# Moving an SSM kernel's parameter columns to a transposing DMA, its stores to ScalarE and one skip product to VectorE

**Chip, cores, metric.** One core of one Trainium2 chip. The metric is the device time of the kernel in microseconds, median of several runs. All results were correct. Starts, waits and clocks are read from one profiled run of each kernel.

## The reference

For 2048 tokens of width 448 (bf16): normalize `x` to `xn`, run a diagonal complex state space model over the tokens, multiply its output by a gate from a gated MLP (1792 hidden columns), add `x`.

```python
xn = layernorm(x)
# A: state space model, 448 complex states
h_t = Lam_bar * h_(t-1) + B_bar @ xn_t            # Lam_bar = exp(exp(log_dt) * Lambda)
s   = 2 * Re(C @ h) + xn * Dskip                  # xn * Dskip is "the skip"
# B: gated MLP
g = silu((silu(xn @ w_gate) * (xn @ w_up)) @ w_down)
out = x + s * g
```

The parameters `log_dt`, `Lambda_re`, `Lambda_im` and `Dskip` are rows of 448 in memory. The kernel needs them as columns, one state to a partition.

## The kernel before

The tokens go through in four blocks of 512 (`q`), each of four tiles of 128 (`j`). The order on TensorE is gate and up products (`gu`, tiles `gp`, `up`), input products of the model (`pb`), output sums (`y`) and down products (`hd`). Where the argument below needs a block, it says pb(2) or hd(1). The recorded texts also call the input products `bu`: the third bu is pb(2). Tile names in the profile: `gs` and `us` are gate and up copied out of PSUM, where TensorE's matmuls write; `Vt` is their product, which the down products read; `sg` is the SiLU of `hd`; `ob` is the output tile; a "notice" is the message between the shares. TensorE runs "cold" when its granted clock shows 0.50, half rate.

The matmul groups. Each contraction is cut into two shares that use two halves of the array (64*128 in the profile; a gate and an up product start together). The program lets the second share of a pair start only when the first share is done. That order goes through GpSimd: an empty instruction there waits for TensorE, and TensorE waits for it.

```python
def tell(mm):
    told = nc.gpsimd.nop(nofuse=True)                       # stands in GpSimd's queue
    tc.add_manual_dep(told.ins, mm.ins.name, SYNC, reason="share")
    return told.ins.name

def sums(q, pairs, between=None):                           # cut
    for share, first in ((0, True), (1, False)):
        for n, two in enumerate(pairs):
            ...                                             # matmuls of this share
                if not first and m == 0:
                    told_of(mm, left[n])                    # second share waits for the notice
            if first:
                left.append(tell(mm))
        if first:
            run_power()                                     # queues one pow on GpSimd
```

The layer norm of later blocks: ScalarE makes the sums (`act_sum`, with tile `junk`), GpSimd the root, on the same queue as those notices.

```python
def act_root(q):                                            # cut
    nc.gpsimd.tensor_scalar(out=vep[...], in0=sums_of[:, 1, :], ...)
    nc.gpsimd.tensor_tensor(out=rstd[...], in0=vep[...], in1=halves[:], op=ALU.pow)
    nc.gpsimd.tensor_tensor(out=off_of[:, 1, :], in0=off_of[:, 0, :], in1=rstd[...], op=ALU.mult)
```

The start, where the parameter columns come out of tile 3's transposes:

```python
def second_tokens():
    ln_evacuate(2, ln_transpose(2), nc.scalar)              # tile 2: PSUM -> xT by ScalarE
    t = ln_transpose(3)
    tv = params_row(t)                                      # six tiny TensorE transposes
    ln_evacuate(3, t, nc.vector)
    nc.scalar.activation(pcol[:], tv, ACT.Copy)             # the columns
    power(dtv[:], euler[:], pcol[:, 0:KT, 0])               # first user, on GpSimd
```

The middle of the program:

```python
    turned_norms(8, 9, 10, 11)                              # ScalarE norms, SyncE transposing DMAs
    outs(0, sg)                                             # outputs of block 0, stores on SyncE
    sg = downs(1, 2.4, {                                    # hd(1)
        0: act_sums((12, 13, 14), 0) + [on(skips, 2)],
        1: act_sums((15,), 0) + [act_means] + act_sums((12, 13), 1),
        2: act_sums((14, 15), 1) + [on(act_root, 3)],
    })
    drive(2, 4.8)                                           # pb(2), scans
    gu(2, bg, 2.4)
```

Of the kernel before, what the change touches and what calls it, by code (L numbers as in the profile page):

```python
# [10 lines left out]
ALU = mybir.AluOpType  # L11
ACT = mybir.ActivationFunctionType
BF16 = mybir.dt.bfloat16
# [31 lines left out]
def kernel(  # L45
# [43 lines left out]
    def blk(k):  # L89
        return slice(k * P, k * P + P) if k < KF else slice(D - P, D)  # L90

    def block(n):
        return slice(n * P, (n + 1) * P)
# [13 lines left out]
    def ctile(shape, dtype, name):  # L107
        return const.tile(shape, dtype, name=name)
# [13 lines left out]
    Id = ctile([P, P], BF16, "Id")  # L122
    CT = ctile([P, KT, W], BF16, "CT")
    ST = ctile([P, KT, W], BF16, "ST")
    vrow = ctile([4, D], BF16, "vrow")
    xn = [ctile([P, KT * P], BF16, f"xn{i}") for i in range(TQ)]
    pcol = ctile([P, KT + 1, 4], F32, "pcol")
    it_f = work.tile([P, W], F32, name="it_f", tag="row", bufs=1)
# [40 lines left out]
    natC = [work.tile([P, KT, D], BF16, name="natC", tag="nz") for _ in range(2)]  # L169
    nc.vector.memset(Wd[:, 0, :], 0.0)  # L170
    nc.vector.memset(Id[:], 0.0)
    nc.vector.memset(half_pi[:], math.pi / 2)
    for h, v in ((slice(0, R), TWO_PI), (slice(R, P), -TWO_PI)):
        nc.vector.memset(two_pi[h], v)

    def warm(n):
        t = bank("warm")
        for _ in range(n):
            nc.tensor.matmul(t[:, 0:D], lhsT=Wd[:, 0, 0:P], rhs=Wd[:, 0, :], start=True, stop=True)
# [51 lines left out]
    vep = ctile([P, NT], F32, "vep")  # L231
    rstd = ctile([P, NT], F32, "rstd")

    def ln_stats(n):
        st = work.tile([P, nc.vector.BN_STATS_DIM], F32, name="st")
        nc.vector.bn_stats(out=st[:], in_=x_all[:, n, :])
        nc.vector.bn_aggr(out=mv[:, n, :], in_=st[:])
        nc.vector.tensor_scalar(
            out=vep[:, n : n + 1], in0=mv[:, n, 1:2], scalar1=1e-5, scalar2=None, op0=ALU.add
        )  # L240
# [15 lines left out]

    sums_of = ctile([P, 2, TQ], F32, "sums_of")
    off_of = ctile([P, 2, TQ], F32, "off_of")

    def act_sum(n, squares):  # L260
        i = n % TQ
# [33 lines left out]
    def ln_transpose(n):  # L295
        tp = bank("tp", BF16)
        for k in range(KT):
            nc.tensor.transpose(tp[:, block(k)], xn[n][:, blk(k)], Id[:])
        return tp

    def ln_evacuate(n, tp, eng):
        tp = tp[:, 0 : KT * P].rearrange("p (k c) -> p k c", k=KT)
        if eng is nc.scalar:
            nc.scalar.activation(xT_of(n), tp, ACT.Copy)  # L304
        else:
            nc.vector.tensor_copy(out=xT_of(n), in_=tp)
# [9 lines left out]
    dtv = vnew("dtv")  # L316
    b_re, b_im, nb_im = vnew("b_re"), vnew("b_im"), vnew("nb_im")

    def transpose_state(out, src, k, ident):

        if k < KF:
            nc.tensor.transpose(out, src[:, blk(k)], ident)
        else:
            for h in (slice(0, R), slice(R, P)):
                nc.tensor.transpose(out[h], src[:, KF * P : D], ident)

    def params_row(t):

        tv = t[:, KT * P : KT * P + 4 * (KT + 1)].rearrange("p (k r) -> p k r", r=4)
        for k in range(KT + 1):  # L330
            if k < KT:
                transpose_state(tv[:, k, :], vrow, k, Id[0:4, 0:4])
            else:
                nc.tensor.transpose(tv[:, k, :], vrow[:, blk(KF)], Id[0:4, 0:4])
        return tv

    def params_in():
        tt, ts = nc.vector.tensor_tensor, nc.vector.tensor_scalar
# [36 lines left out]
    def params_out():  # L375
        tt, ts = nc.vector.tensor_tensor, nc.vector.tensor_scalar
        ab = pcol[:, 0:KT, 1:3].rearrange("p k c -> p c k")
        tt(out=lam[:], in0=lam[:], in1=rcol[:].unsqueeze(1).to_broadcast([P, 3, KT]),
           op=ALU.mult)
        ts(out=lam[:, 1, :], in0=lam[:, 1, :], scalar1=1.0, scalar2=None, op0=ALU.subtract)  # L380
        tt(out=prod[:, 0:2, :], in0=lam[:, 1:3, :], in1=ab, op=ALU.mult)
        tt(out=nb[:, 0, :], in0=prod[:, 0, :], in1=prod[:, 1, :], op=ALU.add)
        tt(out=prod[:, 0:2, :], in0=lam[:, 0:2, :], in1=ab, op=ALU.mult)
        tt(out=nb[:, 1, :], in0=prod[:, 0, :], in1=prod[:, 1, :], op=ALU.subtract)
        tt(out=b_re[:], in0=nb[:, 0, :], in1=rden[:], op=ALU.mult)
        tt(out=b_im[:], in0=nb[:, 1, :], in1=rden[:], op=ALU.mult)
        ts(out=nb_im[:], in0=b_im[:], scalar1=-1.0, scalar2=None, op0=ALU.mult)
# [215 lines left out]
        return sg  # L603

    skip = {}
    SKIPS = [(q, j) for q in (1, 2, 3) for j in range(TQ)][:-1]

    def skips(q):

        skip[q] = work.tile([P, TQ, D], BF16, name="skip", tag="nz")  # L610
        for j in range(TQ):
            for c0, c1, x0 in ((0, KF * P, 0), (KF * P, D, KF * P + R)):
                nc.vector.tensor_tensor(
                    out=skip[q][:, j, c0:c1], in0=xn[j][:, x0 : x0 + c1 - c0],
                    in1=skip["row"][:, c0:c1], op=ALU.mult,
                )

    def out_sum(q, j, k0=0, k1=KT):

# [34 lines left out]
    def on(fn, *args):  # L654
        return lambda: fn(*args)
# [4 lines left out]
        run_power()  # L660
    for n in range(2):
        ln_norm(n)
        ln_evacuate(n, ln_transpose(n), nc.scalar)
        warm(1 + n)
    for n in range(2, TQ):
        ln_stats(n)
        ln_root(n, n + 1)
    run_power()
    powers.append(count_tokens)

    def second_tokens():
        ln_evacuate(2, ln_transpose(2), nc.scalar)
        t = ln_transpose(3)
        tv = params_row(t)
        ln_evacuate(3, t, nc.vector)
        nc.scalar.activation(pcol[:], tv, ACT.Copy)
        power(dtv[:], euler[:], pcol[:, 0:KT, 0])

    CW = W // 2
# [37 lines left out]
    def drive(q, budget):  # L717
        bu_alloc(q)
        bu(q, (0, 1, 2), True, [on(table_sin, 3), params_trig] if q == 0 else ())
        if q == 0:  # L720
            params_out()
        ssm_steps(bg, q)
        bg.run(budget)

    def downs(q, budget, hooks={}, n=TQ):
        sg = []
        for j in range(n):
            sg.append(down(q, j))
            for fn in hooks.get(j, ()):
                fn()  # L730
            bg.run(budget)
        return sg

    def outs(q, sg, hooks={}):
        for j in range(len(sg)):
            finish(q, j, out_sum(q, j), sg[j])
            for fn in hooks.get(j, ()):
                fn()

    def do(fns):  # L740
        for fn in fns:
            fn()

    gu(0, bg, 0.0, {
        0: [*stats(4, 5), on(params_in), on(table_phase, 0)],
# [15 lines left out]
    def act_sums(ns, squares):  # L761
        return [on(act_sum, n, squares) for n in ns]

    gu(1, bg, 2.2, {2: cw(0)[0], 3: cw(0)[1], 4: cw(1)[0], 5: cw(1)[1]})
    drive(1, 4.0)
    sg = downs(0, 1.8, {
        0: cw(2)[0] + cw(3)[0] + act_sums((8, 9), 0),
        1: act_sums((10, 11), 0) + [act_means] + act_sums((8, 9), 1) + cw(2)[1] + cw(3)[1],
        2: act_sums((10, 11), 1) + [on(act_root, 2), on(skips, 1)],
    })  # L770
    bg.finish(0)
    turned_norms(8, 9, 10, 11)
    outs(0, sg)
    sg = downs(1, 2.4, {
        0: act_sums((12, 13, 14), 0) + [on(skips, 2)],
        1: act_sums((15,), 0) + [act_means] + act_sums((12, 13), 1),
        2: act_sums((14, 15), 1) + [on(act_root, 3)],
    })
# [1 line left out]
    gu(2, bg, 2.4)  # L780
    bg.finish(1)
    turned_norms(12, 13, 14, 15)
    outs(1, sg)
    sg = downs(2, 2.4, {1: [on(skips, 3)]})
    drive(3, 4.8)
    gu(3, bg, 2.4)
    bg.finish(2)
# [36 lines left out]
```

## Time and profile before

| | |
|---|---|
| time, median of 3 (range) | 187.45 us (186.88 to 187.54) |
| span of the profiled run | 185.0 us |
| TensorE busy | 177.9 us |
| output sums y(0) start | 72.27 |
| input products pb(2) start | 89.04 |
| last matmul ends | 181.16 |

The last three rows are read from TensorE's timeline, and such starts of groups are the ruler of this document: where the distance between two of them changes, time was lost or won there. The lines that carry the argument on the bound stand in the prediction below. One more view mattered, and the prediction did not read it. It is GpSimd's timeline of the kernel before around pb(2); columns are start, length, engine, line, operation, and in brackets the idle time before it with what ended it.

```profile
88.44 0.39 POOL L274 TENSOR_SCALAR vep<-sums_of 128x4 f32<-128x4 f32 x1 [11.50 <-ACT junk L263]
88.92 1.01 POOL L278 TENSOR_TENSOR rstd<-vep,halves 128x4 f32<-128x4 f32 x1
90.00 0.22 POOL L281 TENSOR_TENSOR off_of<-off_of,rstd 128x4 f32<-128x4 f32 x1
```

GpSimd is almost idle here, yet it stands 11.50 us waiting for ScalarE's sums.

### The profile page before, as it was taken

The page shows a single profiled execution, that of the slowest core. Times are in us where ns is not written, and L with a number is a line of the kernel's source. Part 1 is how long each engine was busy: PE and PEld are TensorE (multiplying, and loading weights), DVE is VectorE, ACT ScalarE, POOL GpSimd, SP SyncE. Part 2 cuts the span into 40 slices and gives each one's busy share as a digit, 9 for nine tenths or more (in the row PEclk, how much of TensorE's full clock was granted, in tenths as well). Part 3 has the DMA queues.
Part 4 walks back from the last instruction along what each step waited for, and adds up shares of the span by engine and source line. Part 5 has one row for each costly group of instructions (what it writes and reads, how often), then busy time and mean ns, then how long its engine had stood idle before and what let it go on. Part 6 is the DMA issues. An engine that isn't in the chain of part 4 may idle for free.

```text
span 185.0 us, 3723 instructions
## 1 busy us (share of the span) xinstructions
PE 177.9 (96%) x1449; PEld 87.8 (47%) x1449; DVE 160.1 (87%) x254; ACT 120.2 (65%) x247; POOL 13.4 (7%) x25
## 2 busy tenths in 40 slices
PE   7899999999999999999999999979999999999991
PEld 3574444544444555555454444535454444455551
DVE  4649799999999999902999999999999999999583
ACT  3247879997789999498499556962259696512110
POOL 7332200000000000600300000000000000000000
PEclk9999999999999999999999999999999999999999
DMA  5899655979200000043100000042100000001111
GB/s 160 209 277 338 124 94 112 132 167 377 101 0 0 5 0 0 0 86 81 50 2 4 2 0 4 0 82 70 62 4 0 0 4 0 0 4 50 50 50 50
DMA packets 26129, 12.71 MB, mean 69 GB/s; under 512 B 16000, under 2 KB 26112, under 8 KB 26112
## 3 DMA queue, kind: packets, MB, share of 16 engines
q1 hardware_dynamic: 24896, 12.06, 25.3%
q10 hardware_dynamic: 1088, 0.41, 0.8%
q8 instruction: 11, 0.18, 0.4%
q14 instruction: 6, 0.05, 0.1%
q0 software_dynamic: 128, 0.00, 0.0%
HBM read 7.23 MB, written 1.84 MB: 49 GB/s over the span
## 4 chain that ended last, share of the span: by engine, by line
PE 67%; DVE 25%; DMA 3%; issue 2%; ACT 1%; POOL 0%; SPq 0%; DVEq 0%
PE gp L455 20%; PE hd L597 16%; PE up L455 15%; PE pb L455 9%; PE y L626 7%; DVE bu_re L527 5%; DVE bu_im L527 4%; DVE tmp L521 2%; DVE Vt L589 2%; DVE ob L648 2%; DMA out_dram<-ob 2%; DVE t L645 2%; DVE H_im L521 2%; DVE ere L521 1%; DMA x_all<-in_A_x_dram 1%
## 5 line engine op out<-in xcount | busy, mean ns | idle before, releaser
L455 PE MATMUL gp<-xT,Wg 64*128 64x512 bf16 (+1 forms) x413 | 85.8, 365 | 0.4 <-ACT xT L304 0.3
L455 PE MATMUL up<-xT,Wu 64*128 64x512 bf16 (+1 forms) x413 | 85.8, 365 | 0.0
L455 PEld LDWEIGHTS <-Wg 64*128 64x128 bf16 x413 | 38.5, 94 | 25.1 <-issue 0.4
L455 PEld LDWEIGHTS <-Wu 64*128 64x128 bf16 x413 | 38.4, 94 | 19.7 <-POOLq L437 0.5
L581 ACT ACTIVATE gs<-gp 128x512 bf16<-128x512 f32 x56 | 33.7, 604 | 19.6 <-PE gp L455 11.7
L597 PE MATMUL hd<-Wd,Vt 128*128 128x448 bf16 x224 | 43.4, 353 | 1.3 <-DVE Vt L589 1.3
L585 ACT ACTIVATE us<-up 128x512 bf16<-128x512 f32 x54 | 32.9, 609 | 0.0
L597 PEld LDWEIGHTS <-Vt 128*128 128x128 bf16 x224 | 21.8, 98 | 22.0 <-DVE Vt L589 1.7
L602 ACT ACTIVATE sg<-hd 128x448 bf16<-128x448 f32 x16 | 8.6, 538 | 25.2 <-PE hd L597 20.6
L455 PE MATMUL pb<-xT,BT 64*128 64x512 bf16 (+1 forms) x224 | 21.9, 349 | 0.0
L648 DVE TENSOR_TENSOR ob<-t,x_all 128x448 bf16<-128x448 f32 (+2 forms) x17 | 10.2, 597 | 8.2 <-DMA out_dram<-ob 7.7
L589 DVE TENSOR_TENSOR Vt<-gs,us 128x2048 bf16<-128x2048 bf16 (+1 forms) x16 | 17.2, 1079 | 0.0
L455 PEld LDWEIGHTS <-BT 64*128 64x128 bf16 x224 | 10.7, 94 | 11.4 <-issue 0.7
L626 PE MATMUL y<-C,H_re 128*128 128x448 bf16 (+2 forms) x68 | 15.7, 342 | 0.0
L527 DVE TENSOR_TENSOR_SCAN bu_re<-rcol,H_re,ere 128x512 bf16<-128x512 f32 x12 | 14.9, 1262 | 0.1
L488 ACT ACTIVATE bu_re<-pb 128x512 bf16<-128x512 f32 (+1 forms) x20 | 10.1, 537 | 2.7 <-PE pb L455 2.6
L626 PE MATMUL y<-C,H_im 128*128 128x448 bf16 (+2 forms) x51 | 11.9, 342 | 0.0
L498 ACT ACTIVATE bu_im<-bu_re 64x512 bf16<-64x512 bf16 x16 | 10.0, 628 | 2.1 <-DVE bu_re L527 1.8
L527 DVE TENSOR_TENSOR_SCAN bu_im<-rcol,H_im,eim 128x512 bf16<-128x512 f32 x9 | 11.4, 1262 | 0.0
L287 ACT ACTIVATE xn<-x_all,off_of,rstd 128x384 bf16<-128x384 bf16 (+1 forms) x16 | 8.1, 588 | 2.8 <-POOL off_of L281 2.8
L521 DVE TENSOR_TENSOR tmp<-bu_im,ST 128x2048 bf16<-128x2048 bf16 x8 | 9.7, 1218 | 0.0
L626 PEld LDWEIGHTS <-H_re 128*128 128x128 bf16 x68 | 6.4, 98 | 6.1 <-issue 0.4
(98 smaller groups left out, 174.5 us busy)
## 6 DMA issues: line engine op xcount, KB each, us to landing
out_dram<-ob SPq DMA_DIRECT2D x15, 112.0 KB, 1.7
Wd<-in_B_w_down_dram SPq DMA_DIRECT2D x1, 1568.0 KB, 9.0
x_all<-in_A_x_dram SPq DMA_DIRECT2D x1, 896.0 KB, 5.5
Wg<-in_B_w_gate_dram SPq DMA_DIRECT2D x2, 384.0 KB, 7.0
Wu<-in_B_w_up_dram SPq DMA_DIRECT2D x2, 384.0 KB, 7.6
x_all<-in_A_x_dram SPq DMA_DIRECT2D x1, 448.0 KB, 5.7
Wg<-in_B_w_gate_dram SPq DMA_DIRECT2D x1, 288.0 KB, 3.1
Wu<-in_B_w_up_dram SPq DMA_DIRECT2D x1, 288.0 KB, 4.2
```

The costliest lines, as they stand in the source:

```text
L455: mm = nc.tensor.matmul(out, lhsT=w[h, d, :], rhs=xT[h, d, q * W + c0 : q * W + c1], start=(first and m == 0), stop=(not first and m == 3 ...
L488: nc.scalar.activation(to, pair[i][0], ACT.Copy)
L498: nc.scalar.activation(out[a], in_[b], ACT.Copy)
L521: nc.vector.tensor_tensor(out=of(out, n), in0=of(a, n), in1=of(b, n), op=op)
L527: nc.vector.tensor_tensor_scan(out=T["b"][c][:, k, :], data0=rcol[:, k : k + 1].to_broadcast([P, W]), data1=T["e"][c][:, k, :], initial=in ...
L581: nc.scalar.activation(gs[:, i + j, :], gp_[:], ACT.Silu)
L585: nc.scalar.activation(us[:, i + j, :], up_[:], ACT.Copy)
L589: nc.vector.tensor_tensor(out=Vt[:, f0 : f0 + n, :], in0=gs[:, 0:n, :], in1=us[:, 0:n, :], op=ALU.mult)
L597: nc.tensor.matmul(hd, lhsT=Vt_of[q][:, fi, j * P : (j + 1) * P], rhs=Wd[:, fi, :], start=(fi == 0), stop=(fi == NF - 1),)
L602: nc.scalar.activation(sg[:], hd, ACT.Silu)
L626: nc.tensor.matmul(y[:, c0:c1], lhsT=h, rhs=C2[:, n, c0:c1], start=(n == 0), stop=(n == NS - 1))
L648: nc.vector.tensor_tensor(out=ob[:], in0=t[:], in1=x_all[:, m, c0:c1], op=ALU.add)
```

## The change

The intent: shorten the start (two banks for token tile 1 so that two engines empty it; no parameter transposes on TensorE), take 16 skip matmuls off TensorE, and stop the outputs from waiting for SyncE's transposing issues. The diff, cut to its core:

```diff
-    vrow = ctile([4, D], BF16, "vrow")
+    vrow = work.tile([16, D], BF16, name="vrow", tag="ob")
+    vcol = ctile([P, KT, 16], BF16, "vcol")
...
-    def params_row(t):                      # six TensorE transposes
+    def turn_params():
+        for k, cols in ((slice(0, KF), slice(0, KF * P)), (slice(KF, KT), blk(KF))):
+            nc.scalar.dma_start(out=vcol[:, k, :], in_=vrow[:, cols], transpose=True)
+    def params_col():
+        ...                                 # four small ScalarE copies vcol -> pcol
...
+    def first_norms():                      # ScalarE makes xn of block 0 again
+        for j in range(TQ):
+            nc.scalar.activation(skip[0][:, j, :], x_all[:, j, :], ACT.Identity,
+                                 bias=off_0[:, j : j + 1], scale=rstd[:, j : j + 1])
...                                          # token tile 1: two banks, ScalarE and VectorE
+    nc.scalar.activation(to[0], tps[0], ACT.Copy)
+    warm(2)
+    turn_params()
+    def second_half():
+        nc.vector.tensor_copy(out=to[1], in_=tps[1])
...
     def second_tokens():
         ln_evacuate(2, ln_transpose(2), nc.scalar)
-        t = ln_transpose(3)
-        tv = params_row(t)
-        ln_evacuate(3, t, nc.vector)
-        nc.scalar.activation(pcol[:], tv, ACT.Copy)
+        ln_evacuate(3, ln_transpose(3), nc.vector)
+        params_col()
...
-    sg = downs(0, 1.8, {                    # budget of scan work queued beside each group
+    sg = downs(0, 1.3, {
-        2: act_sums((10, 11), 1) + [on(act_root, 2), on(skips, 1)],
+        2: act_sums((10, 11), 1) + [on(act_root, 2), on(skip_tile, 0), on(skip_tile, 1),
+                                    first_norms, on(skips, 1)],
+        3: [on(skips, 0)],                  # the skip of block 0 on VectorE
...
-    outs(0, sg)
+    outs(0, sg, nc.scalar)                  # stores by ScalarE
...
-    outs(1, sg)
+    outs(1, sg, nc.scalar)
```

More of the change, by code (lines that the diff above doesn't have):

```diff
@@ L171 @@
     nc.vector.memset(Id[:], 0.0)
+    nc.vector.memset(vrow[:], 0.0)
     nc.vector.memset(half_pi[:], math.pi / 2)
@@ L232, with ln_stats @@
     rstd = ctile([P, NT], F32, "rstd")
-    def ln_stats(n):
+    def ln_stats(n, between=None):
         st = work.tile([P, nc.vector.BN_STATS_DIM], F32, name="st")
         nc.vector.bn_stats(out=st[:], in_=x_all[:, n, :])
+        if between:
+            between()
         nc.vector.bn_aggr(out=mv[:, n, :], in_=st[:])
@@ L258 @@
     off_of = ctile([P, 2, TQ], F32, "off_of")
+    off_0 = ctile([P, TQ], F32, "off_0")
     def act_sum(n, squares):
@@ L317 @@
     b_re, b_im, nb_im = vnew("b_re"), vnew("b_im"), vnew("nb_im")
-    def transpose_state(out, src, k, ident):
-        if k < KF:
-            nc.tensor.transpose(out, src[:, blk(k)], ident)
-        else:
-            for h in (slice(0, R), slice(R, P)):
-                nc.tensor.transpose(out[h], src[:, KF * P : D], ident)
-    def params_row(t):
-        tv = t[:, KT * P : KT * P + 4 * (KT + 1)].rearrange("p (k r) -> p k r", r=4)
-        for k in range(KT + 1):
-            if k < KT:
-                transpose_state(tv[:, k, :], vrow, k, Id[0:4, 0:4])
-            else:
-                nc.tensor.transpose(tv[:, k, :], vrow[:, blk(KF)], Id[0:4, 0:4])
-        return tv
+    def turn_params():
+        for k, cols in ((slice(0, KF), slice(0, KF * P)), (slice(KF, KT), blk(KF))):
+            nc.scalar.dma_start(out=vcol[:, k, :], in_=vrow[:, cols], transpose=True)
+    def params_col():
+        last = vcol[:, KF, 0:4]
+        nc.scalar.activation(pcol[:, 0:KF, :], vcol[:, 0:KF, 0:4], ACT.Copy)
+        nc.scalar.activation(pcol[:, KT, :], last, ACT.Copy)
+        for h in (slice(0, R), slice(R, P)):
+            nc.scalar.activation(pcol[h, KF, :], last[R:P], ACT.Copy)
     def params_in():
@@ L605, with skip_tile @@
     skip = {}
-    SKIPS = [(q, j) for q in (1, 2, 3) for j in range(TQ)][:-1]
+    SKIPS = [(q, j) for q in range(NQ) for j in range(TQ)][:-1]
+    def skip_tile(q):
+        skip[q] = work.tile([P, TQ, D], BF16, name="skip", tag="nz")
     def skips(q):
-        skip[q] = work.tile([P, TQ, D], BF16, name="skip", tag="nz")
         for j in range(TQ):
-            for c0, c1, x0 in ((0, KF * P, 0), (KF * P, D, KF * P + R)):
+            parts = [(0, KF * P, 0), (KF * P, D, KF * P + R)] if q else [(0, D, 0)]
+            for c0, c1, x0 in parts:
+                normed = xn[j][:, x0 : x0 + c1 - c0] if q else skip[q][:, j, :]
                 nc.vector.tensor_tensor(
-                    out=skip[q][:, j, c0:c1], in0=xn[j][:, x0 : x0 + c1 - c0],
-                    in1=skip["row"][:, c0:c1], op=ALU.mult,
-                )
+                    out=skip[q][:, j, c0:c1], in0=normed, in1=skip["row"][:, c0:c1], op=ALU.mult
+                )
+    def first_norms():
+        for j in range(TQ):
+            nc.scalar.activation(
+                skip[0][:, j, :], x_all[:, j, :], ACT.Identity, bias=off_0[:, j : j + 1],
+                scale=rstd[:, j : j + 1],
+            )
     def out_sum(q, j, k0=0, k1=KT):
@@ L662 @@
         ln_norm(n)
-        ln_evacuate(n, ln_transpose(n), nc.scalar)
-        warm(1 + n)
+        if n == 0:
+            ln_evacuate(n, ln_transpose(n), nc.scalar)
+            warm(1)
+    tps = [bank("tp", BF16)[:, 0 : 2 * P] for _ in range(2)]
+    for k in range(KT):
+        nc.tensor.transpose(tps[k // 2][:, block(k % 2)], xn[1][:, blk(k)], Id[:])
+    to = [xT_of(1)[:, 2 * i : 2 * i + 2, :] for i in range(2)]
+    tps = [tp.rearrange("p (k c) -> p k c", k=2) for tp in tps]
+    nc.scalar.activation(to[0], tps[0], ACT.Copy)
[3 more added lines that the diff above has]
+        nc.vector.tensor_copy(out=to[1], in_=tps[1])
     for n in range(2, TQ):
-        ln_stats(n)
+        ln_stats(n, second_half if n == 2 else None)
         ln_root(n, n + 1)
@@ L721, in drive @@
             params_out()
+            nc.vector.scalar_tensor_tensor(
+                out=off_0[:], in0=mv[:, 0:TQ, 0], scalar=-1.0, in1=rstd[:, 0:TQ],
+                op0=ALU.mult, op1=ALU.mult,
+            )
         ssm_steps(bg, q)
@@ L732, in downs, with outs @@
         return sg
-    def outs(q, sg, hooks={}):
+    def outs(q, sg, eng=nc.sync):
         for j in range(len(sg)):
-            finish(q, j, out_sum(q, j), sg[j])
-            for fn in hooks.get(j, ()):
-                fn()
-    def do(fns):
-        for fn in fns:
-            fn()
+            finish(q, j, out_sum(q, j), sg[j], eng)
     gu(0, bg, 0.0, {
@@ L772 @@
     turned_norms(8, 9, 10, 11)
-    outs(0, sg)
+    outs(0, sg, nc.scalar)
     sg = downs(1, 2.4, {
-        0: act_sums((12, 13, 14), 0) + [on(skips, 2)],
+        0: act_sums((12, 13, 14), 0) + [on(skip_tile, 2), on(skips, 2)],
         1: act_sums((15,), 0) + [act_means] + act_sums((12, 13), 1),
@@ L782 @@
     turned_norms(12, 13, 14, 15)
-    outs(1, sg)
-    sg = downs(2, 2.4, {1: [on(skips, 3)]})
+    outs(1, sg, nc.scalar)
+    sg = downs(2, 2.4, {1: [on(skip_tile, 3), on(skips, 3)]})
     drive(3, 4.8)
```

## The prediction

> **What bounds the kernel now.** I read the busy table first, then the chain of work that ended last, the waits, the timelines of single engines (start, and 60 to 126 us), and the list of DMA issues.
>
> ```profile
> PE 177.9 (96%) x1449; PEld 87.8 (47%) x1449; DVE 160.1 (87%) x254; ACT 120.2 (65%) x247; POOL 13.4 (7%) x25
> ...
> PE 67%; DVE 25%; DMA 3%; issue 2%; ACT 1%; POOL 0%; SPq 0%; DVEq 0%
> ```
>
> TensorE is busy for 177.9 of 185.0 us and holds 67% of the chain, so a microsecond saved elsewhere counts only where TensorE waits. By stretches of 2 us it is full from 12 to 122 us and again from 126 to 180 us. It waits in two places: the first 11 us, and the end of the third down projection:
>
> ```profile
> PE hd L597 <- DVE Vt L589: 1.3, 1, 1.3
> ...
> DVE ob L648 <- DMA out_dram<-ob: 7.7, 1, 7.7
> ```
>
> The second line (also from the waits) is the origin of the first. VectorE stops from 79.1 to 86.7 us because the two output buffers are full, and their stores stand on SyncE behind four transposing issues:
>
> ```profile
> 78.09 5.13 SPq L309 DMA_TRANSPOSE xT<-xn  x4
> 83.32 5.83 SPq L649 DMA_DIRECT2D out_dram<-ob  x4
> ...
> 86.74 0.63 DVE L648 TENSOR_TENSOR ob<-t,x_all 128x448 bf16<-128x448 f32 x1 [7.68 <-DMA out_dram<-ob]
> ```
>
> (Start, length, engine; in brackets the idle time before.) From there VectorE runs without a gap until it hands TensorE the last Vt at 124.5 us, 1.3 us late.
>
> The start, from the timelines of TensorE, ScalarE and VectorE:
>
> ```profile
> 6.46 0.60 ACT L304 ACTIVATE xT<-tp 128x512 bf16<-128x512 bf16 x1 [0.26 <-PE tp L298]
> ...
> 7.11 0.27 PE L455 MATMUL gp<-xT,Wg 64*128 64x256 bf16 x1 [0.31 <-ACT xT L304]
> ...
> 9.62 0.60 ACT L304 ACTIVATE xT<-tp 128x512 bf16<-128x512 bf16 x1 [2.56 <-PE tp L298]
> ...
> 10.01 0.17 PE L334 MATMUL tp<-Id,vrow 4*128 4x4 bf16 x1
> ...
> 10.22 0.42 DVE L306 COPY xT<-tp 128x512 bf16<-128x512 bf16 x1 [0.90 <-PE tp L334]
> ...
> 10.68 0.19 ACT L676 ACTIVATE pcol<-tp 128x20 f32<-128x20 bf16 x1 [0.47 <-DVE xT L306]
> ...
> 10.70 0.09 PEld L455 LDWEIGHTS <-Wg 64*128 64x128 bf16 x1 [0.36 <-DVE xT L306]
> ```
>
> The first real matmul (7.11) waits for token tile 1's copy out of PSUM. The next restart (10.70) waits for tile 3's copy, itself held by the parameter transposes sharing its bank. After 10.70 TensorE is the path.
>
> [...] each of the four transposing issues above holds SyncE about 1.2 us, pitch 1.3 us[...] (1.24 us for 64 rows too).
>
> [...]
>
> [...] The trace shows the two rates (128x448 matmuls at a pitch of 0.37 us during warm-up, 0.19 us later)[...].
>
> **The change part by part.** Times are on the clock of the kernel before, until the sum.
>
> (a) Second token tile in two banks. ScalarE needs only the first two transposes; VectorE takes the other half after its running bn_stats. By scaling 0.60 and 0.42 us to half width (estimate, 0.35 and 0.25) both end near 6.8: about 0.3 us off the 7.11. Taken alone it is real.
>
> (b) Parameters. Six tiny TensorE transposes go, so tile 3's copy could start near 9.85 instead of 10.22: another 0.4 us. But two transposing issues now stand on ScalarE, *ahead of tile 2's copy out of PSUM*[...]. The built program's semaphore waits, which can be read without running it, are the heart of this prediction. [...] The first new transpose needs, besides the parameter rows, the landing of this load:
>
> ```profile
> 7.08 0.43 SPq L143 DMA_DIRECT2D Wu<-in_B_w_up_dram  x1
> ...
> Wu<-in_B_w_up_dram SPq DMA_DIRECT2D x1, 288.0 KB, 4.2
> ```
>
> Issued at 7.08, landed at 7.08 + 4.2 = 11.3. That such landings gate issues is visible before: SyncE's last Wu issue stands at 13.78, which is the x load's 8.09 + 5.7. So the first transpose issues at 11.3, the second at 11.3 + 1.3 = 12.6 (its load has landed by about 12.1), ending 13.8. Tile 2's copy then runs 13.85 to 14.45, and TensorE restarts near 14.5 instead of 10.70: **+3.8 us**. Part (a) vanishes inside this wait, and so does a small loss: the third Wu issue on ScalarE now waits for an x load and moves from 3.70 to about 5.35.
>
> Next on ScalarE, before the first SiLU, stand the pcol copies. The second transpose lands 2.4 us (the xT transposes' figure) to 4.0 us (BT's worst) after 12.6, so at 15.0 to 16.6; three copies of about 0.2 us follow. TensorE will want the first SiLU's bank near 16.5. I add 0.3, in sum **+4.1 us**.
>
> (c) Skip of the first 512 tokens on VectorE. Sixteen matmuls leave TensorE. One output sum takes 1.52 us with them (73.39, 74.91, 76.43 in the chain) and 1.34 without (the row at 173.00): 4 x 0.18 = **-0.7 us**, on the path.
>
> (d) VectorE and the stores. ScalarE makes four normed tiles: from 73.68, about 0.6 us each, pitch 0.55, last at 76.0. VectorE has finished the other queued work near 72.1, so it waits 2.2 us and finishes the four products (0.38 each) at 76.35. One ere (1.13) leads to 77.5. Four finishes of three operations follow: in the second block such four took 124.46 to 132.45, so 8.0, until 85.5. They no longer wait for stores: ScalarE is through with its normalization at 81.0, issues store 0 then, and the buffer is free by about 83.1, when the third tile needs it. Skip products for the next block (1.5) and the deferred tmp and ere (2 x 1.24) end at 89.5; before, the scans began at 90.19. Of 7.7 us of idle time removed, 7.0 are spent on new or moved work and waits. From the scans to the last Vt the new order holds 32.1 us (7 scans 8.4, H 6.3, the next ere and eim 6.4, 6 scans 7.1, four Vt 4.0): 121.6. TensorE reaches it at 123.2 - 0.7: the wait goes, **-1.3 us**.
>
> (e) ScalarE behind the stores. It must wait for the fourth finish (85.5), so the SiLU of the next down projection moves from 81.20 to 86.0. Its work up to the fourth SiLU is 7.2 us: 93.2. TensorE wants that bank for the eighth pb at 89.04 - 0.7 + 3.0 + 0.9 = 92.2. A stall of up to 1.0; I count **+0.6 us**.
>
> Sum: 4.1 - 0.7 - 1.3 + 0.6 = +2.7. The median of 187.45 becomes **190.1 us**.
>
> The tail is unchanged: VectorE waited 1.9 us for y at 174.36, and keeps that slack.
>
> **The rivals.** *The start is not held* (the load lands sooner, or the issues are short): then (a) and (b) give about -0.7, and with the rest the sum is -2.1, 185.3 us. For it: the intent, and parameters being needed only near 15.7 us, when VectorE reads dtv. Against it: a named semaphore and a load whose landing is known. *The array goes cold*: TensorE idles from about 10.4 to 14.5 us, 4.1 us[...]. [...] *VectorE becomes the bound*: it gets 4.1 us of extra operations (1.55 products, 2.5 additions). If its 2.2 us wait for the normed tiles were doubled, the scans would start 1.5 us later than before, and the Vt wait would stay: about 191.5. *The stores stall TensorE more*: if the fourth finish is 2 us later, the pb bank is too, so (e) becomes 2.6 and the result 192.
>
> **Range and chances.** Held start without cold array: 190.1, give or take 1. I give the held start 85%, and within it the cold array 25%. Range 187.0 to 193.0. Faster needs under 183.7, below even the first rival: 3%. Slower needs over 191.2: mostly the cold cases plus a late tail of the others, 27%. Within 2%: 70%.
>
> **What will show it.** ScalarE's two transposing issues near 11.3 and 12.6 us with tile 2's copy after them; a TensorE gap of about 4 us ending near 14.5 with that copy as releaser; y at 1.34 us per sum in the first block; no VectorE wait for a store near 80 us, one of about 2 us for normed tiles instead; no wait for Vt at the third down projection; ScalarE's SiLU late by about 5 us after the first outputs. I am wrong if those issues stand before 10 us, if TensorE restarts before 12 us, or if matmuls after the gap have the pitch of the warm-up.

The sum came to +2.7 us, 190.1 us.

## The result, and the profile after

The changed kernel takes **198.32 us** (197.76 to 198.68, 4 runs) against 187.42 for the kernel before on the same chip: ratio 1.0585, 95% interval 1.0548 to 1.0622. Ratios here are the mean time of one kernel's fast runs over that of the other's of the same rounds, so they are not quite the ratio of the medians. Executions over 1.5% slower than the fastest of the same kernel are left out of the means. All outputs are right. The prediction had 190.1 and a range that ended at 193.0.

The changed kernel's page, its busy times, granted clock and chain:

```profile
PE 180.4 (92%) x1427; PEld 91.2 (47%) x1427; DVE 165.1 (84%) x265; ACT 122.9 (63%) x254; POOL 12.9 (7%) x25
...
PEclk9975999999999999999988999999999999999999
...
PE 71%; ACT 9%; DVE 8%; DMA 4%; issue 2%; ACTq 1%; POOL 1%; SPq 1%; DVEq 0%; POOLq 0%
```

TensorE has 22 instructions fewer and is busy 2.5 us longer. The clock row says why: it drops in slices 3 and 4 and again around slice 21, and before it was 9 throughout. Both places are where TensorE waits, in the list of its waits:

```profile
PE pb L454 <- POOLq L436: 5.5, 1, 5.5
PE gp L454 <- ACT xT L309: 4.9, 1, 4.9
```

(Total, times, longest.) The second is the held copy that the prediction named. The first, a wait of pb(2) for GpSimd's queue, it did not name. The ruler, starts of TensorE's groups:

| | before | after | shift | time added since the row above |
|---|---|---|---|---|
| pb(0) | 29.82 | 35.90 | +6.1 | +6.1 |
| hd(1) | 78.35 | 83.66 | +5.3 | -0.8 |
| gu(2) | 94.35 | 106.69 | +12.3 | +7.0 |
| pb(3) | 133.03 | 143.93 | +10.9 | -1.4 |
| last matmul ends | 181.16 | 192.06 | +10.9 | 0.0 |

So the changed kernel's two small gains are there (-0.8 and -1.4), and two losses outweigh them.

**The start**, from the timelines of ScalarE, TensorE and GpSimd after:

```profile
11.72 2.47 ACTq L326 DMA_TRANSPOSE vcol<-vrow  x2
14.24 0.60 ACT L309 ACTIVATE xT<-tp 128x512 bf16<-128x512 bf16 x1 [7.44 <-issue]
...
14.89 0.37 PE L454 MATMUL gp<-xT,Wg 64*128 64x256 bf16 x1 [4.91 <-ACT xT L309]
...
17.54 0.21 ACT L331 ACTIVATE pcol<-vcol 128x12 f32<-128x12 bf16 x1 [2.70 <-DMA vcol<-vrow]
...
18.95 1.02 POOL L224 TENSOR_TENSOR dtv<-euler,pcol 128x4 f32<-128x4 f32 x1 [9.21 <-PE up L454]
```

The two issues hold ScalarE from 11.72, the copy comes at 14.24, TensorE restarts at 14.89. These three are within half a microsecond of the prediction. Then the columns come late, at 17.5, and the first user of them on GpSimd starts at 18.95; in the list of DMA issues the two transposes took 5.5 us to land. In this run the columns do not hold TensorE: what released GpSimd at 18.95 is TensorE's own notice (`<-PE up`), and no wait of TensorE stands there. But TensorE restarts at half rate, as the table by stretches says (busy time and count of TensorE first; the granted clock stands before the last two columns):

```profile
12.00:14.00 2.00, 0.00 (x0) 0.00 (x0) 0.00 (x0) 0.00 (x0) 0.00 (x0) 0.60 1.09 375
14.00:16.00 2.00, 1.11 (x12) 0.93 (x13) 0.00 (x0) 0.60 (x1) 0.00 (x0) 0.50 1.10 356
16.00:18.00 2.00, 2.00 (x22) 1.67 (x20) 0.57 (x1) 0.21 (x1) 0.00 (x0) 0.50 1.14 290
```

**The middle**, from the timelines of ScalarE, GpSimd and TensorE after:

```profile
87.96 4.50 ACTq L659 DMA_DIRECT2D out_dram<-ob  x3
92.51 0.54 ACT L601 ACTIVATE sg<-hd 128x448 bf16<-128x448 f32 x1 [5.68 <-DVE ob L658]
...
99.20 0.42 POOL L279 TENSOR_SCALAR vep<-sums_of 128x4 f32<-128x4 f32 x1 [17.56 <-ACT junk L268]
99.71 1.90 POOL L283 TENSOR_TENSOR rstd<-vep,halves 128x4 f32<-128x4 f32 x1
101.69 0.29 POOL L286 TENSOR_TENSOR off_of<-off_of,rstd 128x4 f32<-128x4 f32 x1
...
101.73 1.89 PE L454 MATMUL pb<-xT,BT 64*128 64x512 bf16 x8 [5.48 <-POOLq L436]
```

Read it upwards. TensorE goes on 0.04 us after GpSimd has begun the third operation of `act_root(3)`; the notice between the shares stood behind it. GpSimd had waited for ScalarE's sums. ScalarE makes them after its SiLU at 92.51, and that SiLU stood behind the three stores, which wait for VectorE's last output. TensorE wanted the notice at 101.73 - 5.48 = 96.25, 1.9 us after pb(2) began at 94.34. In the kernel before the same point is 89.04 + 1.9 = 90.9, and GpSimd was in its third operation at 90.00: a slack of 0.9 us that no row of waits shows (an expectation below counts it to the operation's end at 90.22 and says 0.7).

### The profile page after: what moved, and what is told of

It reads as the page before. It is cut to its first block, busy times and chain, and to the rows that moved or that the text cites. A ratio compares the mean times of both kernels' runs of the same rounds, so it can differ in the third digit from the quotient of the medians.

```text
span 195.8 us, 3697 instructions
## 1 busy us (share of the span) xinstructions
PE 180.4 (92%) x1427; PEld 91.2 (47%) x1427; DVE 165.1 (84%) x265; ACT 122.9 (63%) x254; POOL 12.9 (7%) x25
## 4 chain that ended last, share of the span: by engine, by line
PE 71%; ACT 9%; DVE 8%; DMA 4%; issue 2%; ACTq 1%; POOL 1%; SPq 1%; DVEq 0%; POOLq 0%
PE gp L454 25%; PE up L454 19%; PE hd L596 11%; PE pb L454 11%; PE y L636 6%; ACT junk L268 5%; DVE t L655 3%; DVE ob L658 3%; DMA Wu<-in_B_w_up_dram 2%; DVE t L653 2%; DMA Wg<-in_B_w_gate_dram 2%; ACT skip L623 1%; ACTq L326 1%; ACT c_tb L418 1%; ACT sg L601 1%
## 5 line engine op out<-in xcount | busy, mean ns | idle before, releaser
L454 PE MATMUL gp<-xT,Wg 64*128 64x512 bf16 (+1 forms) x413 | 87.8, 372 | 5.0 <-ACT xT L309 4.9
L454 PE MATMUL up<-xT,Wu 64*128 64x512 bf16 (+1 forms) x413 | 87.7, 372 | 0.0
L454 PEld LDWEIGHTS <-Wg 64*128 64x128 bf16 x413 | 39.6, 96 | 24.6 <-issue 0.6
L454 PEld LDWEIGHTS <-Wu 64*128 64x128 bf16 x413 | 39.5, 96 | 23.3 <-issue 4.7
L580 ACT ACTIVATE gs<-gp 128x512 bf16<-128x512 f32 x56 | 33.7, 603 | 14.5 <-PE gp L454 14.4
L454 PE MATMUL pb<-xT,BT 64*128 64x512 bf16 (+1 forms) x224 | 23.4, 364 | 5.5 <-POOLq L436 5.5
L454 PEld LDWEIGHTS <-BT 64*128 64x128 bf16 x224 | 11.6, 97 | 17.6 <-POOLq L436 6.0
L636 PE MATMUL y<-C,H_re 128*128 128x448 bf16 (+2 forms) x68 | 15.1, 342 | 0.0
L653 DVE TENSOR_TENSOR t<-y,skip 128x448 f32<-128x448 f32 x15 | 9.3, 623 | 3.2 <-PE y L636 2.0
L655 DVE TENSOR_TENSOR t<-t,sg 128x448 f32<-128x448 f32 x15 | 9.4, 625 | 0.8
```

Source lines behind the costliest of these rows:

```text
L454: mm = nc.tensor.matmul(out, lhsT=w[h, d, :], rhs=xT[h, d, q * W + c0 : q * W + c1], start=(first and m == 0), stop=(not first and m == 3 ...
L580: nc.scalar.activation(gs[:, i + j, :], gp_[:], ACT.Silu)
L636: nc.tensor.matmul(y[:, c0:c1], lhsT=h, rhs=C2[:, n, c0:c1], start=(n == 0), stop=(n == NS - 1))
L653: nc.vector.tensor_tensor(out=t[:], in0=y, in1=skip[q][:, j, c0:c1], op=ALU.add)
L655: nc.vector.tensor_tensor(out=t[:], in0=y, in1=sg[:, c0:c1], op=ALU.mult)
```

## The experiments

Sixteen kernels ran, in four groups on a chip each; the kernel before ran beside them at 187.1 to 187.3.

### Undo each loss, and both

`params_by_pe` is the changed kernel with the columns made by TensorE again. `root_late` moves only `act_root(3)`, behind the notices it stood before. `both_mended` has both edits.

```diff
-        2: act_sums((14, 15), 1) + [on(act_root, 3)],
+        2: act_sums((14, 15), 1),
...
-    gu(2, bg, 2.4)
+    gu(2, bg, 2.4, {1: [on(act_root, 3)]})
```

> The changed kernel with one part undone: the parameter columns come from TensorE transposes again, as before. Theory (held start): ScalarE's two transposing issues at 11.7 us held tile 2's copy, and the 4.9 us gap also threw the array to half rate; both go, 6.1 us together, plus some tenths from the two-bank split: about 192 us, the first bu matmul near 29.6 us instead of 35.9, and the 5.5 us wait of the third bu still there. Rival (the weight loads hold TensorE at the start): the restart stays near 14.9 us and the time near 198.

> The changed kernel with one move: GpSimd's three operations for the fourth block's layer norm (which wait for ScalarE's sums) are queued after the third bu instead of before it. Theory (relay): the third bu's second half waits for a notice that TensorE sends by way of GpSimd, and GpSimd stood on the layer norm until 101.7 us; with the move the 5.5 us wait and the half rate after it (1.5 us) go, leaving at most 1.3 us of wait for the bank that ScalarE's late fourth SiLU frees: 191 to 193 us. Rival (the bank, as I had predicted): TensorE waits for ScalarE's SiLU in any case, and the time stays within 1 us of 198.3.

> The two edits before together. If the two losses are separate and add, 198.3 - 6.3 - 6.0 = 186 (185 to 187), that is about 1 us under the kernel before; if one hides the other, it is above 188.

Measured: 193.13 (ratio 1.0311, 1.0279 to 1.0343), 192.04 (1.0261, 1.0233 to 1.0290) and 186.54 (0.9963, 0.9939 to 0.9986). In `params_by_pe` the wait for `xT` is gone, pb(0) starts at 29.41 and the wait for GpSimd's queue stays at 5.5. In `root_late` it is the other way round. With both, the only long wait that is left in the block loop is the one that the prediction had counted with 0.6 us, in the waits of `both_mended`:

```profile
PE pb L458 <- ACT sg L605: 1.1, 1, 1.1
```

So the two losses are separate, and together they are all of it.

### Which parts make the loss in the middle

Each is the kernel before with only the parts named: `only_stores` (stores on ScalarE), `only_skip` (skip of block 0 on VectorE), `stores_skip` (both).

```diff
-    outs(0, sg)                       # only_stores, stores_skip; the same for outs(1, sg)
+    outs(0, sg, nc.scalar)
...
+        2: ... first_norms, on(skips, 1)],   # only_skip, stores_skip
+        3: [on(skips, 0)],
```

> The kernel before with only the stores moved to ScalarE's queue. Relay theory: ScalarE's sums for act_root(3) come late, GpSimd is through with the layer norm at about 94 us, where TensorE needs its notice at about 90.9: a wait of pb or gp for GpSimd's queue of 3 to 4 us, perhaps 1.5 of cold clock behind it, the wait of hd(2) for Vt gone (-1.3), the bank stall behind the SiLU about 1: 189.5 to 192 us. Rival (the stores cost only the bank stall, and the wait needed the skip on VectorE): 187 us, no wait for GpSimd's queue.

> The kernel before with the skip alone on VectorE, stores on SyncE's queue. Relay theory: ScalarE is not held by stores, but its four extra operations (2.7 us) push its sums some 2 us back, past the 0.7 us of slack: a wait for GpSimd's queue of 1 to 2.5 us; hd(1) shorter by 0.8; VectorE's outputs later, so hd(2)'s wait for Vt grows from 1.3 to 2 to 3.5 us: 188.5 to 191 us. Rival (the skip alone harms nothing): 186.7, no wait for GpSimd's queue.

> The kernel before with the stores on ScalarE's queue and the skip on VectorE together, columns and banks as before. The stores alone cost nothing (only 0.3 us of wait for GpSimd's queue). Theory: the loss needs both, since VectorE's skip makes the outputs late and ScalarE, holding the stores, waits for those outputs ahead of its sums: the wait of pb for GpSimd's queue of about 5.5 us is there in full, 192.5 to 193.7 us, as with the columns mended. Rival (a third part is needed, or the columns' delay shifted things): under 189.

Measured: `only_stores` **186.36** (0.9943, 0.9907 to 0.9979), `only_skip` **186.73** (0.9991, 0.9955 to 1.0028), `stores_skip` **193.04** (1.0321, 1.0289 to 1.0353). The first two expectations were misses: neither part harms alone. Together they lose about 6 us, as much as the kernel with the columns mended, so the two banks have no share in it. The timelines show the interaction. VectorE's last output of the four, and GpSimd's third operation, in `only_stores`:

```profile
81.02 0.63 DVE L648 TENSOR_TENSOR ob<-t,x_all 128x448 bf16<-128x448 f32 x1 [0.49 <-DMA out_dram<-ob]
...
91.08 0.29 POOL L281 TENSOR_TENSOR off_of<-off_of,rstd 128x4 f32<-128x4 f32 x1
```

and in `stores_skip` VectorE's first skip product, the same output, ScalarE's stores and GpSimd's third operation:

```profile
74.31 0.39 DVE L618 TENSOR_TENSOR skip<-skip,skip_row 128x448 bf16<-128x448 bf16 x1 [1.75 <-ACT skip L625]
...
85.23 0.63 DVE L660 TENSOR_TENSOR ob<-t,x_all 128x448 bf16<-128x448 f32 x1
...
81.73 4.50 ACTq L661 DMA_DIRECT2D out_dram<-ob  x3
...
95.46 0.29 POOL L282 TENSOR_TENSOR off_of<-off_of,rstd 128x4 f32<-128x4 f32 x1
```

With the stores alone, the outputs come early enough that ScalarE issues them between its normalizations (0.36 us each) and waits 1.0 us for the last; GpSimd is 1.1 us later than before and uses up the slack. The skip on VectorE waits for ScalarE's tiles, adds an operation to each output, and makes the last output 4.2 us later (85.23 against 81.02). That delay reaches TensorE only because ScalarE stands in line for the output ahead of its sums. In `only_skip` the stores are on SyncE, ScalarE does not stand, and its third GpSimd operation starts at 88.92, before it is needed. My error in that expectation was to add ScalarE's 2.7 us of new tiles to a chain that had idle time ahead of it.

### What makes the loss at the start

`only_params` is the kernel before with the columns by DMA alone.

> The kernel before with only the transposing columns added. Theory: the two transposing issues hold ScalarE ahead of tile 2's copy as in the changed kernel, and the second of them stands behind a completion semaphore that the 448 KB load of x fulfils here at some 13.2 to 13.8 us, so TensorE takes up tile 2 at about 15.5 us, and pb(0) starts 6 to 7 us later than before; no other loss: 193.5 to 195 us. Rival (the start's loss needs the other parts beside it, for example the two banks): under 191. If the issues run back to back, restart near 14.9 and 193.5.

Measured 192.37 (1.0252, 1.0205 to 1.0299); pb(0) at 37.32, so the start's loss needs no other part. The time fell below the expected band because the delay of TensorE also removes its wait for Vt: hd(2) to pb(3) takes 10.7 us instead of 12.1.

Three bonds were proposed for it: the held copy, the half rate after the gap, and the late landing. `start_fill` keeps TensorE busy with 36 products of zeros; `fill_notice` also adds a place in GpSimd's queue, so that the second pair's notices stand ahead of the user of the columns, and puts the first work on the columns (`params_in`, `table_phase`) one group later.

```diff
+    fill(36)                                   # start_fill, fill_notice: zeros into an unused half bank
...
+        powers.append(lambda: None)            # fill_notice
         power(dtv[:], euler[:], pcol[:, 0:KT, 0])
...
-        0: [*stats(4, 5), on(params_in), on(table_phase, 0)],     # fill_notice
+        0: stats(4, 5),
+        1: [on(params_in), on(table_phase, 0)],
```

> The changed kernel with 36 matmuls on zeros (0.11 us each) put into TensorE's gap at the start, written where the next real matmuls overwrite them. Theory (the array went cold in the gap): the restart stays at 14.9 us, but the matmuls after it run at full rate from the first, and 1.9 us come back: 196.4. Rival (the slow matmuls after the restart wait for weights): nothing changes, 198.3.

> The kernel with the zero products in the start gap, and the GpSimd operation that needs the columns put behind the second pair's notices. Theory (half rate and the late columns bind side by side, either alone hides the other): the wait of 1.15 us for GpSimd's queue goes, and the full rate now pays: 196.5 to 197.5 us. Rival (another wait binds there too): 198.5 still.

Measured: 198.66 (fast runs; 1.0603, 1.0577 to 1.0628) and 199.28 (1.0613, 1.0563 to 1.0664). Both miss. The full rate is there and gains nothing (pb(0) at 35.80 in `start_fill`, and 36.71 in `fill_notice`, whose issues took 3.73 us), because in `start_fill` GpSimd's queue takes over; the GpSimd operation and the matmul that goes on 0.05 us after its start:

```profile
19.65 1.02 POOL L224 TENSOR_TENSOR dtv<-euler,pcol 128x4 f32<-128x4 f32 x1 [9.62 <-ACT pcol L334]
...
19.70 0.28 PE L454 MATMUL up<-xT,Wu 64*128 64x256 bf16 x1 [1.15 <-POOLq L436]
```

With that notice moved (`fill_notice`) a third wait appears, 1.2 us of a gate product for ScalarE's `gs`: ScalarE stands 2.33 and 1.39 us before its copies of the columns too, and its first `gs` comes after them, at 20.95.

`copy_first` puts the two issues behind tile 2's copy; `cols_behind` does that, moves `act_root(3)`, and puts everything that uses the columns two groups later.

```diff
-    turn_params()
...
         ln_evacuate(2, ln_transpose(2), nc.scalar)
+        turn_params()
```

> The changed kernel with the two transposing issues moved behind tile 2's copy on ScalarE, all else as changed. Theory (the held copy is not the only bond of the start: the late landing binds beside it, through the GpSimd operation that needs the columns and stands ahead of the second pair's notices): TensorE takes up tile 2 at about 11, stands again from about 14 until about 19.7 for GpSimd's queue, pb(0) starts at 34.5 to 36 (changed kernel 35.9), 197 to 198.5 us. Rival (the held copy and its cold clock are the start's loss): pb(0) at 30 to 31, about 193.

> The changed kernel with act_root(3) moved, the transposing issues behind tile 2's copy, and all that needs the columns (their copies on ScalarE, the GpSimd operations, the phases) two to three groups later. Theory: hold and landing are all of the start's loss, so the columns by a transposing DMA cost nothing here and the time is that of the kernel with both mended, 186.0 to 187.2 us, pb(0) at 29.3 to 30.3. Rival (the transposing traffic or the later phases cost something more): pb(0) past 31, over 187.5.

Measured: **213.04** (1.1385, 1.1357 to 1.1414) and **203.88** (1.0907, 1.0884 to 1.0930). Both edits failed as experiments on the size of the loss, and showed something else. From the timeline of ScalarE and the waits of TensorE in `copy_first`:

```profile
28.14 2.45 ACTq L326 DMA_TRANSPOSE vcol<-vrow  x2
...
PE up L454 <- POOLq L436: 19.0, 1, 19.0
```

The issues now stand at 28.14. SyncE's transposing loads of B, whose issues begin at 18.03, come first, and the chain that ended last runs through them (on the page of `copy_first`: SPq L159 3%, DMA BT 1%); why ScalarE's issues wait for them was not shown. Tile 2's copy ran at 9.83, so nothing was held by it, and TensorE still stood 19.0 us for GpSimd's queue. That shows the bond by the landing, though at a landing that the edit had moved. In `cols_behind` ScalarE itself stood at that issue and TensorE waited 16.5 us for `gs`.

The last group separates the three, each with `act_root(3)` moved, so against `root_late`. `land_only` issues the two transposes on SyncE, ahead of its last four weight loads, and loads the parameter rows earlier on GpSimd so that they are there. `hold_cold` leaves them on ScalarE but puts the users of the columns two groups later. `hold_full` adds the zeros to that. `cols_sync` has these issues on SyncE and the users later, with the stores split as in the next experiment.

```diff
-    landed = load_gu(768, 1280)
+    landed = load_gu(768, 1280)
+    turn_params()                              # land_only, cols_sync: on nc.sync
     load_gu(1280, F)
...                                              # the rows' loads to vrow moved up (cut)
-        0: [*stats(4, 5), on(params_in), on(table_phase, 0)],     # hold_*, cols_sync
-        2: [*stats(6, 7), *root(1), on(table_sin, 0)],
+        0: stats(4, 5),
+        1: [params_cols],
+        2: [*stats(6, 7), *root(1), on(params_in), on(table_phase, 0)],
...                                              # table_sin(0) one group later as well (cut)
```

> The changed kernel with act_root(3) moved and the two transposing issues on SyncE's queue, ahead of its last four weight loads, instead of on ScalarE; all that uses the columns stands where the change put it. ScalarE's copy of tile 2 is not held (restart at 10.7 to 11.2). Theory (the late landing is a bond of its own): the columns land at 15 to 17.5, the GpSimd operation and ScalarE's copies of the columns hold TensorE for 2.5 to 5 us, pb(0) at 32.5 to 35 (changed 35.9, before 29.8), 189 to 191.5 us. Rival (the landing costs nothing without the hold): pb(0) at 29.4 to 30.5, 186.5.

> The changed kernel with act_root(3) moved, the issues on ScalarE as changed, everything that uses the columns two groups later, and 36 zero products in the start gap so that TensorE keeps its full rate: the hold alone. Theory: restart at 14.5 to 15.5, pb(0) later than before by just that hold, 33.5 to 34.8, 190 to 191.3 us. Rival (half rate is not the third bond): pb(0) at 35.5 or later, 192.

> The same without the zero products: hold and half rate, no late columns. Theory: half rate alone takes what the columns took, pb(0) at 35.3 to 36.2 as in the changed kernel, 191.7 to 192.5 us. Rival (the columns alone were the loss beyond the hold): pb(0) at 33.5 to 34.8, 190.5.

> The issues on SyncE's queue, the users of the columns two groups later, act_root(3) moved, the stores split between ScalarE (first two tiles) and SyncE (last two). Theory: neither hold nor landing binds, the start is as before: pb(0) at 29.4 to 30.5, no wait for GpSimd's queue, no wait for xT over 0.4 us, 184.3 to 185.5 us, as fast as the mended kernel with split stores. Rival (the held SyncE delays weight loads or the transposing loads of B): pb(0) past 31, over 186.

| | bonds left | time (ratio, interval) | pb(0) starts |
|---|---|---|---|
| `root_late` | hold, half rate, landing | 192.04 (1.0261) | 35.76 |
| `land_only` | landing (and half rate after its own gap) | 193.91 (1.0365, 1.0326 to 1.0403) | 37.80 |
| `hold_cold` | hold, half rate | 192.46 (1.0277, 1.0241 to 1.0313) | 36.37 |
| `hold_full` | hold | 191.33 (1.0223, 1.0184 to 1.0261) | 34.78 |
| `cols_sync` | none | 184.42 (0.9852, 0.9829 to 0.9876) | 30.12 |

`land_only`, from the timelines of ScalarE, GpSimd and TensorE:

```profile
9.43 0.60 ACT L314 ACTIVATE xT<-tp 128x512 bf16<-128x512 bf16 x1 [2.56 <-PE tp L308]
17.96 0.21 ACT L332 ACTIVATE pcol<-vcol 128x12 f32<-128x12 bf16 x1 [7.94 <-DMA vcol<-vrow]
...
18.98 1.02 POOL L229 TENSOR_TENSOR dtv<-euler,pcol 128x4 f32<-128x4 f32 x1 [9.18 <-ACT pcol L335]
...
19.04 0.39 PE L455 MATMUL up<-xT,Wu 64*128 64x256 bf16 x1 [5.90 <-POOLq L437]
```

The copy is on time, the columns are not, and TensorE stops 5.90 us for the notice and then goes on cold (the clock row of its page shows 0.5 in the slice from 19.2 to 24.0 us). The late landing is a bond of its own, and worth more than I expected, since the clock fell in its gap as well. `hold_full` against the 29.82 of before makes the hold alone 5.0 us; `hold_cold` makes hold and half rate 6.6. The difference, 1.6, understates the half rate, because the issues took 3.36 us in `hold_full` and 2.47 in `hold_cold`, so that TensorE restarted at 15.87 and at 14.70. From the restart to pb(0) it is 18.9 us in `hold_full`, 19.1 in the kernel before, 21.7 in `hold_cold` and 21.0 in the changed kernel: the half rate cost 2.8 us in `hold_cold` and 1.9 in the changed kernel. (These are single profiled runs; the times of `hold_full`, 190.44 to 192.26, and of `hold_cold`, 191.44 to 193.07, overlap.) The stretch from 16 to 18 us shows it, first in `hold_cold`, then in `hold_full`:

```profile
16.00:18.00 2.00, 2.00 (x22) 1.61 (x20) 0.76 (x2) 0.68 (x2) 0.00 (x0) 0.50 1.07 298
```

```profile
16.00:18.00 2.00, 2.00 (x38) 1.89 (x36) 0.73 (x2) 0.70 (x2) 0.00 (x0) 1.00 1.13 264
```

The same 2 us of busy TensorE hold 22 matmuls at half rate and 38 at full. So the half rate comes on top of the hold, and the landing lies beside the half rate and did not add to it: `root_late`, which has all three, starts pb(0) at 35.76, and `hold_cold`, without the landing, at 36.37. Behind a hold, the landing shows only when the half rate is taken away, as a wait of 1.15 us in `start_fill`.

### A version that beats both

`split_stores` is `both_mended` with the last two stores of each output stretch back on SyncE, so that ScalarE does not stand in line for the late outputs.

```diff
-            finish(q, j, out_sum(q, j), sg[j], eng)
+            finish(q, j, out_sum(q, j), sg[j], eng if j < 2 else nc.sync)
```

> The mended kernel (columns by TensorE, act_root(3) moved) with the first two row tiles' stores of the first two output stretches by ScalarE and the last two by SyncE. Theory: the first SiLU of gu(2) no longer waits behind all stores, the bank stall of 1.1 us is gone, and the wait for Vt stays away: 185.2 to 185.8 us. Rival (the stall is taken over by another wait of the same length): 186.5.

Measured 184.72 (0.9872, 0.9835 to 0.9910). pb(2) to gu(2) takes 5.3 us instead of 6.6 in `both_mended`, so the stall for the bank is gone and no other took its place there. The profiled run, at 185.79 one of the two slower of the six, shows the same kind of chain through GpSimd's queue once more, at the start: VectorE waits 1.46 us for an x load, GpSimd waits for VectorE, and a notice in GpSimd's queue holds TensorE 1.10 us (pb(0) at 30.72, against 29.46 in `both_mended`):

```profile
17.30 1.19 POOL L222 TENSOR_TENSOR rcol<-euler,zr 128x4 f32<-128x4 f32 x1 [4.44 <-DVE zr L347]
17.33 0.39 PE L458 MATMUL up<-xT,Wu 64*128 64x512 bf16 x1 [1.10 <-POOLq L440]
```

`cols_sync` has the same stores and keeps the columns on the DMA: 184.42. Both are faster than the kernel before by 1.3 and 1.5%, with intervals well apart from 1; the two are not told apart. In `cols_sync` the columns still land late, at 18.67, but nothing that TensorE waits for stands behind them:

```profile
11.64 2.45 SPq L163 DMA_TRANSPOSE vcol<-vrow  x2
...
18.67 0.21 ACT L332 ACTIVATE pcol<-vcol 128x12 f32<-128x12 bf16 x1 [2.84 <-DMA vcol<-vrow]
```

## Why the prediction was wrong, step by step

The prediction summed +2.7 us; TensorE's ruler shows +10.9. The difference of 8.2 is +2.0 in (b), +6.4 in (e), and -0.1 each in (c) and (d).

- **(a) two banks.** Foreseen to vanish inside the start's wait. Not run alone, but `stores_skip` and `params_by_pe`, which differ in nothing but the banks, are at 1.0321 and 1.0311 of the kernel before.
- **(b) columns.** The mechanism of the hold was right: the semaphore of a weight load set the issue (the load landed at 7.19 + 4.4 = 11.6, ScalarE's semaphore instruction ahead of the issue stands at 11.6 and the issue at 11.72, said 11.3), ScalarE's copy stood behind it, TensorE restarted at 14.89 (said 14.5), so the hold was 4.2 (said 3.8). What failed is the term after it, 0.3 us for the late columns: from the restart to pb(0) TensorE lost 1.9. In the changed kernel that was the half rate, which the prediction had put aside as a rival with a chance of one in four. That chance was the author's estimate, and far too low: in all five profiled runs with a gap of 4.3 to 5.9 us at the start, and in the two with 16.5 and 19.0, the clock fell; in the three whose gap the zeros cut to 1.2 to 2.3 us it stayed at 1.00. The columns were mis-sized beside it: the landing was taken as 2.4 to 4.0 us from other transposes of the trace, and it took 5.5, in a stretch where the DMA engines were full (share 1.05 to 1.14) and the ordinary loads beside it took 4.3 to 6.1. With the half rate taken away they cost 1.15 (`start_fill`), not 0.3.
- **(c) skip off TensorE.** Right: -0.8 against -0.7.
- **(d) VectorE.** Right in mechanism: no wait for a store near 80 us, and the wait for Vt gone, -1.4 against -1.3. In the changed kernel that number alone proves nothing, and its agreement is partly luck: TensorE came so late that the wait would have gone anyway, as in `only_params`, where VectorE still stands 6.27 us for a store. `only_stores` settles it: pb(0) is on time there, and hd(2) to pb(3) takes 10.7 us instead of 12.1. VectorE's waits for ScalarE's normed tiles were 2.5 us, said 2.2. (The five parts of the prediction's 32.1 us add up to 32.2.)
- **(e) ScalarE behind the stores. This is the step that failed.** Its first half was right: ScalarE's SiLU came at 92.51, which without the 6.1 us of the start is 86.4, said 86.0. The step then followed that lateness to one consumer only, the PSUM bank of the next pb, and counted +0.6. The bank is real, and where nothing else is in the way it costs 1.1. But the same late ScalarE makes the sums for `act_root(3)`, GpSimd waits for them in order, and the notice between the two shares of pb(2) stands behind. That came first and cost 7.0: 5.5 of wait, and about 1.5 of half rate after it (the clock stood at 0.50 from about 101 to 104.5 us). Some 0.9 of the 5.5 is the pow of `act_root(3)` itself, 1.90 us here and 1.01 before. Moving `act_root(3)` alone takes it away.

ScalarE and GpSimd took up their work in the program's order at every point of this chain, and where a notice stood behind an operation that waited, it cost TensorE 5.5 us in the middle and 5.9 at the start of `land_only`. I had counted with that order for ScalarE and not asked which other queues hold something of TensorE's. TensorE was released 0.03 to 0.06 us after the operation ahead of the notice had begun (0.03 in `split_stores`, 0.04 in the middle of the changed kernel, 0.05 in `start_fill`, 0.06 in `land_only`), so it did not wait for that operation's end, but for all that the operation waited for. Nor was the time to issue a DMA small: the two column transposes held ScalarE for 2.5 us in the changed kernel, beside 5.5 to land.

What stays open: how much of the start each bond would cost without the others in the changed kernel itself (the landing hides behind the half rate, and the issues' length varied from 2.4 to 3.7 us between the kernels), why the clock fell sooner after some gaps than after others (counted from TensorE's last matmul, 1.9 us in `root_late`, 2.4 in the changed kernel's start (9.98 to 12.4), 4.5 in `land_only` and 4.9 in the changed kernel's middle; the ends of matmuls are modelled in the profile, so a tenth or two of this is loose), and why the pow of `act_root` took 1.0 us in some runs and 1.9 in others.

## What to carry to other kernels

Before moving work onto an engine, list everything that stands behind it in that engine's queue, and then everything that stands behind the consumers in *their* queues; an engine that is 7% busy can carry the one instruction that the bounding engine waits for, and its slack is on no page until it is used up. Two moves that each cost nothing alone can share one slack, so the parts of a change should be tried in pairs, not only singly. For a transfer's landing, take the loads that are in flight at that time as the measure, not the same operation elsewhere in the trace. Here the two column transposes took 5.5 us beside loads of 4.3 to 6.1, with the DMA engines full (share 1.05 to 1.14), where transposes of xT took 2.5. From their first issue to ScalarE's first copy of the columns it was 5.8 us (11.72 to 17.54); in `copy_first`, at a DMA share of about 0.1, it was 2.5 (28.14 to 30.64).
